# Attention by head pairs in 64-row halves of TensorE, the mask as a product, and the mixer spread over the next batch's attention steps

## The chip, the cores and the metric

The kernel runs on one core of one Trainium2 chip. The metric is the time of one execution on the device, in microseconds; lower is better. "TensorE" does matrix products, "VectorE" and "ScalarE" elementwise work, "GpSimd" copies and most DMA issues. A run is "fast" unless it lies more than 1.5% above the fastest of its kernel; only fast runs enter the ratios.

## The reference, cut to what matters

Four batches, 8 heads, 768 tokens, 64 columns a head: block-sparse attention, then a two-layer token and channel mixer on the 512 concatenated columns.

```python
scores = scale * np.matmul(q, k.transpose(0, 1, 3, 2))
# mask: neighbouring 32-token blocks, first and last block, and sampled blocks
scores = np.where(mask, scores, -1000000000.0)
attn = np.exp(scores - scores.max(-1))            # then divided by its row sum
x    = attn @ v                                    # (4, 768, 512), heads side by side

a1  = alpha1 * x + beta1
u   = x + lam * np.einsum('ts,bsd->btd', w_tok, a1)
a2  = alpha2 * u + beta2
out = u + lam * (np.maximum(a2 @ w_ch1, 0.0) @ w_ch2)
```

The scores are small (q and k have a spread of 0.1), so exponentials need no maximum.

## The kernel before: the parts that the change touches

Attention runs head by head in 192 steps (32 heads, 6 key tiles). One step is two QK products, one exponential on ScalarE and two PV products. The mask is inside the QK product: 24 extra contraction rows (88 instead of 64) carry block indicators and a large negative number. PV leaves the result with head columns on the partitions, so `emit_finish` transposes it back in fp32.

```python
def emit_qk(i, jt):
    ...
    nc.tensor.matmul(spsum[:, 0:512], kT[0 : D + NBLK, ts(jt, P)],
                     qT[0 : D + NBLK, 0:512], start=True, stop=True)
    nc.tensor.matmul(spsum[:, 512:S], ...)
    nc.scalar.activation(eT[:], spsum[:], AF.Exp, bias=expb[:], scale=SCALE)

def emit_pv(i, jt):
    ...
    nc.tensor.matmul(opsum[0 : D + 1, 0:512], vext[:, jt, :], eT[:, 0:512], ...)
    nc.tensor.matmul(opsum[0 : D + 1, 512:S], vext[:, jt, :], eT[:, 512:S], ...)
    ...                                  # after 6 key tiles: copy to otsb

def emit_finish(i):                      # 6 fp32 transposes, reciprocal, product
    ...

for g in range(NBH * NT + PVD):          # attention of ALL batches
    ...
nc.gpsimd.dma_start(w2b[:], ...)
nc.vector.tensor_mul(out=w2b[:], in0=w2b[:], in1=lam...)     # one product of 8192 columns
for b in range(B): ...                   # then the mixer of ALL batches
for c in range(NT): ...
```

The softmax here doesn't subtract the row's maximum and nothing guards it: scores larger than these inputs give would overflow.

## Time and profile before

| | before |
|---|---|
| median of the runs | 440.7 us |
| span of the profiled run | 436.4 us |
| first exponential | 13.7 us |
| last exponential | 203.5 us |
| step in the window 60 to 120 us | 0.91 us (66 exponentials in 60 us) |
| last exponential to the end (mixer) | 233 us |

The first fence has the busy times and the slices of the page. Each digit is the busy share of one fortieth of the span (about 11 us) in tenths; PEclk is TensorE's granted clock in tenths of full.

```profile
PE 387.7 (89%) x2175; PEld 211.5 (48%) x2196; DVE 189.1 (43%) x404; ACT 214.8 (49%) x289; POOL 83.9 (19%) x107
...
PE   0699489799989999898589999999999999999996
...
DVE  4345465876577567854945530311401301302101
ACT  1389469689977999696000043062060260440520
...
PEclk9999879989998999999989999999999999999999
```

The ACT row tells the structure: ScalarE is at 6 to 9 in most slices up to the nineteenth (attention), then mostly idle, while the PE row stays at 8 or 9 nearly to the end. Two phases stand one after the other: attention, paced by the exponentials, and the mixer, paced by TensorE.

The second fence is the window view of the attention (60 to 120 us) and of the hand-over (205 to 220 us). Each engine has its busy time and, in brackets, its instructions; the last columns are granted clock, DMA share and GB/s.

```profile
60.00:120.00 60.00, 56.63 (x394) 36.18 (x393) 39.55 (x97) 53.31 (x66) 26.85 (x34) 0.97 0.86 55
205.00:220.00 15.00, 6.93 (x54) 4.04 (x53) 13.96 (x30) 0.00 (x0) 0.00 (x0) 0.99 0.00 0
```

In the attention ScalarE is busy 53.3 of 60 us. Its mean record is 0.906 us, but records overlap a little: 53.3 us over 66 is 0.81 us a step, and in an unbroken run the starts are 0.78 to 0.80 us apart. In the hand-over TensorE works 6.9 of 15 us.

The third fence is from the waits of VectorE. Its columns: who waited, for what, microseconds in total, times, the longest.

```profile
DVE w2b L328 <- DMA w2b<-in_moe_w_ch_dram: 6.6, 1, 6.6
```

VectorE stands 6.6 us for the second channel weight, which lands at 50.1 us, and then needs 4.4 us to scale it.

### The profile page before, as it was taken

How to read it: one execution, taken by the hardware profiler on the slowest of the kernel's cores; microseconds unless marked ns; L12 is line 12 of the kernel's file. 1: busy time of each engine (PE TensorE's matmuls, PEld its weight loads, DVE VectorE, ACT ScalarE, POOL GpSimd, SP SyncE). 2: the span in 40 equal slices, each digit the busy share in tenths (PEclk: the TensorE clock that was granted, in tenths of full speed). 3: DMA queues.
4: the chain of work that ended last, by engine and by line, in shares of the span. 5: the costliest groups of instructions: out<-in, count | busy, mean ns of one | idle time of the engine just before them, and what ended most of it. 6: DMA issues, size and time to landing. Idle time of an engine off the chain costs nothing.

```text
span 436.4 us, 5598 instructions
## 1 busy us (share of the span) xinstructions
PE 387.7 (89%) x2175; PEld 211.5 (48%) x2196; DVE 189.1 (43%) x404; ACT 214.8 (49%) x289; POOL 83.9 (19%) x107
## 2 busy tenths in 40 slices
PE   0699489799989999898589999999999999999996
PEld 0366256456655666465234454444544544544442
DVE  4345465876577567854945530311401301302101
ACT  1389469689977999696000043062060260440520
POOL 9436234244443544210000000000000000000000
PEclk9999879989998999999989999999999999999999
DMA  9999949769984999520000000200101101001001
GB/s 129 183 208 154 166 29 63 47 43 64 59 55 29 66 62 59 33 19 2 0 2 0 0 2 16 82 0 26 72 0 50 49 2 72 24 2 73 23 26 72
DMA packets 84149, 22.46 MB, mean 51 GB/s; under 512 B 77140, under 2 KB 80156, under 8 KB 84124
## 3 DMA queue, kind: packets, MB, share of 16 engines
q0 software_dynamic: 78928, 14.96, 41.3%
q1 hardware_dynamic: 5196, 7.15, 4.8%
q8 instruction: 17, 0.28, 0.3%
q14 instruction: 8, 0.07, 0.0%
HBM read 30.77 MB, written 6.29 MB: 85 GB/s over the span
## 4 chain that ended last, share of the span: by engine, by line
PE 69%; DVE 11%; DMA 8%; POOL 4%; ACT 3%; issue 3%; another core or an unknown queue 1%; ACTq 0%; DVEq 0%; POOLq 0%
PE hps L377 18%; PE chps L390 18%; PE spsum L218 8%; PE tokps L345 7%; PE opsum L242 7%; PE opsum L249 3%; DMA w2b<-in_moe_w_ch_dram 3%; PE spsum L225 3%; DMA qk<-in_k_dram 2%; DMA vext<-in_v_dram 2%; ACT eT L233 2%; PE txp L206 2%; PE xps L268 2%; POOL qk L187 2%; DVE otsb L258 1%
## 5 line engine op out<-in xcount | busy, mean ns | idle before, releaser
L233 ACT ACTIVATE eT<-spsum,expb 128x768 f16<-128x768 f32 x192 | 156.9, 906 | 45.2 <-PE opsum L249 21.3
L384 ACT ACTIVATE hts<-hps 128x512 bf16<-128x512 f32 x96 | 56.7, 597 | 158.1 <-PE hps L377 158.1
L377 PE MATMUL hps<-a2t,w1b 128*128 128x512 bf16 x374 | 85.8, 379 | 1.5 <-ACT hts L384 0.5
L390 PE MATMUL chps<-w2b,hts 128*128 128x512 bf16 x376 | 83.3, 379 | 0.4
L242 PE MATMUL opsum<-eT,vext 128*65 128x512 f16 x192 | 75.2, 399 | 6.3 <-DVE vext L194 5.4
L399 DVE TENSOR_TENSOR ot<-x_sb,chps 128x512 f32<-128x512 f32 x24 | 16.5, 687 | 142.6 <-PE chps L390 139.8
L390 PEld LDWEIGHTS <-hts 128*128 128x128 bf16 x384 | 37.6, 98 | 45.3
L377 PEld LDWEIGHTS <-w1b 128*128 128x128 bf16 x384 | 37.6, 98 | 42.7 <-issue 2.5
L249 PE MATMUL opsum<-eT,vext 128*65 128x256 f16 x192 | 54.2, 282 | 0.0
L206 PE MATMUL txp<-identb,qk 128*128 128x128 bf16 x192 | 26.5, 232 | 22.3 <-DMA qk<-in_k_dram 14.8
L258 DVE COPY otsb<-opsum 65x768 f32<-65x768 f32 x32 | 30.5, 954 | 28.3 <-PE opsum L249 27.9
L184 POOL DMA_DIRECT2D qk<-in_q_dram x32 | 26.5, 829 | 63.5 <-PE txp L206 61.3
L191 POOL DMA_DIRECT2D vext<-in_v_dram x32 | 26.5, 828 | 40.4 <-PE opsum L249 31.6
L206 PEld LDWEIGHTS <-qk 128*128 128x128 bf16 x192 | 17.0, 104 | 32.8 <-DMA qk<-in_q_dram 14.0
L242 PEld LDWEIGHTS <-vext 128*65 128x65 f16 x192 | 22.1, 115 | 16.7 <-issue 3.1
L249 PEld LDWEIGHTS <-vext 128*65 128x65 f16 x192 | 22.1, 115 | 11.7 <-issue 7.9
L218 PE MATMUL spsum<-qText_65,kText_68 88*128 88x512 bf16 x66 | 26.4, 401 | 0.8 <-ACT eT L233 0.6
L187 POOL DMA_DIRECT2D qk<-in_k_dram x32 | 26.7, 834 | 0.0
L218 PE MATMUL spsum<-qText_66,kText_69 88*128 88x512 bf16 x66 | 25.6, 388 | 0.8 <-ACT eT L233 0.5
L345 PEld LDWEIGHTS <-wtokT 128*128 128x128 bf16 x144 | 14.4, 100 | 24.5 <-issue 7.7
L218 PE MATMUL spsum<-qText_67,kText_70 88*128 88x512 bf16 x60 | 23.1, 386 | 1.4 <-ACT eT L233 1.4
L353 DVE TENSOR_TENSOR x_sb<-x_sb,tokps 128x512 f32<-128x512 f32 x24 | 16.4, 687 | 15.3 <-PE tokps L345 15.3
(62 smaller groups left out, 336.7 us busy)
## 6 DMA issues: line engine op xcount, KB each, us to landing
out_dram<-ot SPq DMA_DIRECT2D x24, 256.0 KB, 2.0
qk<-in_q_dram POOLq DMA_DIRECT2D x32, 96.0 KB, 3.0
qk<-in_k_dram POOLq DMA_DIRECT2D x32, 96.0 KB, 3.3
vext<-in_v_dram POOLq DMA_DIRECT2D x32, 96.0 KB, 3.2
w1b<-in_moe_w_ch_dram POOLq DMA_DIRECT2D x1, 2048.0 KB, 14.0
w2b<-in_moe_w_ch_dram POOLq DMA_DIRECT2D x1, 2048.0 KB, 14.5
wtk<-in_moe_w_tok_dram POOLq DMA_DIRECT2D x1, 1152.0 KB, 10.3
lam_bc<-in_moe_lam_dram SPq DMA_DIRECT2D x1, 256.0 KB, 3.6
```

The source lines that it names most:

```text
L184: nc.gpsimd.dma_start(qk[:, :, 0:D], q[b, h].rearrange("(o p) d -> p o d", p=P))
L187: nc.gpsimd.dma_start(qk[:, :, D:P], k[b, h].rearrange("(o p) d -> p o d", p=P))
L206: nc.tensor.transpose(tps[:, j, :], qk[:, 3 * g + j, :], identb[:])
L218: nc.tensor.matmul(spsum[:, 0:512], kT[0 : D + NBLK, ts(jt, P)], qT[0 : D + NBLK, 0:512], start=True, stop=True,)
L233: nc.scalar.activation(eT[:], spsum[:], AF.Exp, bias=expb[:], scale=SCALE)
L242: nc.tensor.matmul(opsum[0 : D + 1, 0:512], vext[:, jt, :], eT[:, 0:512], start=(jt == 0), stop=(jt == NT - 1),)
L249: nc.tensor.matmul(opsum[0 : D + 1, 512:S], vext[:, jt, :], eT[:, 512:S], start=(jt == 0), stop=(jt == NT - 1),)
L258: nc.vector.tensor_copy(out=otsb[0 : D + 1, :], in_=opsum[0 : D + 1, :])
L345: nc.tensor.matmul(tokps[:], wtokT[:, sk, ts(tt, P)], a1pp[:, sk, :], start=(sk == 0), stop=(sk == NT - 1),)
L377: nc.tensor.matmul(hps[:], w1b[:, dk, ts(ntl, P)], a2t[:, dk, :], start=(dk == 0), stop=(dk == 3),)
L384: nc.scalar.activation(hts[:, ntl, :], hps[:], AF.Relu, bias=0.0, scale=1.0)
L390: nc.tensor.matmul(chps[:], hts[:, nk, ts(m, P)], w2b[:, nk, :], start=(nk == 0), stop=(nk == 15),)
```

## The change

Its intent: (1) one step now serves a *pair* of heads and half of the query tokens, with each head's 64 contraction rows in its own half of TensorE's rows, so that the two QK products can run side by side; (2) the mask becomes a 0/1 factor on the exponentials, multiplied by VectorE; (3) PV makes tokens the output rows, six products of 65 columns, so no transpose back is needed; (4) the mixer of batch b is cut into small pieces and woven into the attention steps of batch b+1, and only the last mixer stands alone; (5) larger DMA runs. The core of the diff (cuts marked; lines of indexing are left out):

```diff
-            nc.tensor.matmul(spsum[:, 0:512], kT[0 : D + NBLK, ts(jt, P)], ...)
-            nc.tensor.matmul(spsum[:, 512:S], kT[0 : D + NBLK, ts(jt, P)], ...)
-            nc.scalar.activation(eT[:], spsum[:], AF.Exp, bias=expb[:], scale=SCALE)
+        for a in range(2):
+            nc.tensor.matmul(
+                sps[:, a, 0:HS],
+                kT[a * D : (a + 1) * D, ts(jt, P)],
+                qT[a * D : (a + 1) * D, ts(hf, HS)],
+                start=True,
+                stop=True,
+            )
+        eT = wk.tile([P, 2, HS], F16, name="eT", tag="eT", bufs=5)
+        nc.scalar.activation(eT[:], sps[:, :, 0:HS], AF.Exp, bias=expb[:], scale=SCALE)
+        nc.vector.tensor_tensor(
+            out=eT[:],
+            in0=eT[:],
+            in1=mask[:, jt, ts(hf, HS)].unsqueeze(1).broadcast_to([P, 2, HS]),
+            op=ALU.mult,
+        )
 ...
-            nc.tensor.matmul(opsum[0 : D + 1, 0:512], vext[:, jt, :], eT[:, 0:512], ...)
-            nc.tensor.matmul(opsum[0 : D + 1, 512:S], vext[:, jt, :], eT[:, 512:S], ...)
+        for a in range(2):
+            for t in range(3):
+                nc.tensor.matmul(
+                    op[:, a, t, 0 : D + 1],
+                    eT[:, a, ts(t, P)],
+                    vx[:, a, jt, 0 : D + 1],
+                    ...
+                )
 ...
+    def mm_tile(shape, dt=FP):          # everything but scores and PV shares two buffers
+        return ps.tile(shape, dt, name="mm", tag="mm", bufs=2)
 ...
+    fill = setup()                      # wtok transposes, bias products, 8 pieces of w2b
+    for i in range(len(steps) + LAG):   # 192 steps
+        emit_qk(steps[i])
 ...
+            if pos == MIXLAG and b > 0:
+                ...
+                fill = mixer(b - 1)
+                rate = 52000.0 / PER
 ...
+        emit_pv(steps[i - LAG])
 ...
+        credit += rate
+        while credit > 0:               # so much of the mixer (or setup) per step
+            c = next(fill, None)
 ...
+    for _ in mixer(B - 1):
+        pass
```

## The prediction

> **What bounds the kernel before (span 436.4 us).** The profile has three parts.
> (a) 0 to about 55 us: start and a stall. The first exponential runs at 13.7 us. In the timeline the product that scales w2b sits in VectorE's queue and waits 6.6 us for its DMA (landing 50.1 us), then takes 4.4 us; the chain of waits shows that DMA as one 14.5 us piece.
> (b) about 55 to 205 us: attention, bound by ScalarE. In the window 60 to 120 us it ran 66 exponentials in 60 us (0.91 us a step) and was busy 53.3 us; inside an unbroken run one costs about 0.81 us. TensorE has slack but cannot use it: the mixer comes later.
> (c) about 205 to 432 us: the mixer, bound by TensorE (chain: hps, chps, tokps). N=512 matmuls start every 215 ns; 912 of them are 196 us, plus transposes, a 15 us hand-over at 205 to 220 us and an output tail of 4 us.
>
> **What the change does.** It puts three of the four mixers among the attention steps of the next batch, so (b) and (c) overlap. Costs on TensorE, from start-to-start times in the trace:
> - QK: two 384-column products in 64-row halves. The Trainium skill ("TensorE: Matmul & The Clock Gate", Part 3) says such tiles run concurrently, so 165 ns instead of 320; but "TensorEngine Tiling (Array Packing)", Key Properties, says a mode switch drains the engine, twice a step. No trace here shows either; I estimate 315 ns a step in all: no gain.
> - PV: six 65-column matmuls, each with a new 128-column weight load. The trace shows 55 ns start to start for bf16 128x128 load and transpose; I estimate 45 ns, 270 ns a step against 323.
> - The otsb copies and fp32 transposes (0.95 us and 6 x 62 ns a head) vanish.
> - Mixer matmuls cost the same (512 of 163 ns, 384+144 of 215 ns).
> Sum over the new instruction order: TensorE about 335 us.
>
> VectorE gains 192 mask products (fp16, 768 columns). The w2b product ran at 0.54 ns a column, so 0.4 to 0.56 us each, about 95 us; it stays near 57 us a batch. ScalarE gets 39 us of exponentials and about 17 us of 384-column relus a batch. Both stay under TensorE's roughly 80 us a batch, so batches 1 to 3 are bound by TensorE, with small bubbles because all mixer products share two PSUM buffers and relus queue behind exponentials.
>
> **Where time is lost.** Loads have 1536-byte reads instead of 256, but six memsets and two relayout copies on GpSimd precede the first product: first exponential at 15 to 18 us. In the new instruction order the first w2b product again stands early in VectorE's queue, after about 12 steps, and w2b is issued third behind wtk and w1b: I expect VectorE, then all engines, to stall from about 28 us until about 53 us. Batch 0 has no mixer to fill it.
>
> **Sum:** batch 0 ends near 90 us; batches 1 to 3 take 240 us; the last mixer 58 us; bubbles and output tail 8. About 396 us.
>
> Faster by over 2%: 0.91; within 2%: 0.05; slower: 0.04. Range 368 to 425 us.
>
> **Right or wrong shows in:** slices (TensorE near 9 from about 90 us on, ScalarE at 6 to 8); VectorE's wait for w2b; start-to-start of PV (45 ns) and of a QK pair (under 20 ns if concurrent) and the gap at the QK-PV change; the mask product's mean; VectorE idle in batches 1 to 3.
>
> **What would make it wrong:** PV at 60 ns or more or longer drains (+25 us); VectorE slower because GpSimd contends, becoming the bound; bubbles on the two shared buffers; or, on the other side, free mode switches and 30 ns PV (about 360 us).

## The result, and the profile after

| | before | after |
|---|---|---|
| median | 439.52 us (437.89 to 441.76) | 420.71 us (415.14 to 421.97) |
| ratio after / before | | 0.9513, 95% interval 0.9435 to 0.9591 |
| span of the profiled run | 436.4 us | 418.6 us |

A ratio here is the mean time of one kernel's fast runs over that of the other's fast runs of the same rounds, so it is not quite the ratio of the two medians. The 421.97 us run counted as slow by the 1.5% rule. The change gained 4.9%; the prediction had 396.0 us, a gain of 10%.

The busy times and slices of the page after (a slice is 10.5 us):

```profile
PE 370.4 (88%) x2951; PEld 186.2 (44%) x2978; DVE 259.3 (62%) x498; ACT 235.0 (56%) x321; POOL 69.6 (17%) x93
...
PE   0489299799799999998899999999999999789996
...
DVE  5886366988985584579854854699548546820101
ACT  1035246776448769754478599445785992044350
...
PEclk9999999757989999999899999999999999999999
```

TensorE has 8 or 9 in every slice from the twelfth to the last mixer, as intended, and ScalarE is spread out. TensorE's holes are in the first eleven slices (the 2 in the fifth is the stall on w2b), and VectorE, 43% busy before, is 62% busy and stands at 8 or 9 for more than one slice at regular places: slices 8 to 12, then 19 and 20, then 27 and 28, around the starts of the mixers of batches 0, 1 and 2 (slices 2 and 3 are the start of the kernel; 15, 23, 31 and 35 stand alone).

A second reading uses the start of every exponential, taken from the trace. There are 48 a batch, so the 49th begins batch 1. The sum of the prediction can be laid beside it:

| part | predicted | measured | difference |
|---|---|---|---|
| batch 0 (to the 49th exponential) | 90 | 98.0 | +8.0 |
| batches 1 to 3 (to the last exponential) | 240 | 251.7 | +11.7 |
| last mixer, bubbles and output tail | 66 | 68.9 | +2.9 |
| execution outside the profiled span | 0 | 2.1 | +2.1 |
| sum | 396 | 420.7 | +24.7 |

(The last row but one is 420.7 us less the span of 418.6 us.) The prediction gave its 8 us of "bubbles and output tail" as one sum; the table puts all of it in the third row, although some of the bubbles were meant for batches 1 to 3, so that the second difference may be a few us smaller and the third larger. Either way both large misses are in the attention.

The window view, with the windows cut at the first w2b product, the 49th and the last exponential:

```profile
49.20:98.00 48.80, 43.18 (x403) 23.84 (x402) 37.23 (x77) 30.06 (x34) 11.30 (x15) 0.80 0.35 52
98.00:349.70 251.70, 243.20 (x2072) 121.20 (x2095) 170.15 (x331) 172.15 (x240) 30.31 (x39) 0.98 0.18 35
```

In batches 1 to 3 TensorE is busy 243.2 of 251.7 us, so a first glance says "bound by TensorE". Keep in mind that products are pipelined and the ends of their records are modelled, so a busy TensorE is not one at its peak; the experiments show below that a part of these 243 us goes without any change to its products.

The waits of VectorE, with the same columns as before:

```profile
DVE eT L234 <- ACT eT L233: 72.5, 84, 1.5
...
DVE w2b L403 <- DMA w2b<-in_moe_w_ch_dram: 8.0, 1, 8.0
```

The wait for w2b is the predicted one: VectorE reaches the first w2b product at 41.2 us and stands 8.0 us until 49.2 us. The next fence, pieces of the chain of waits of batch 0 (start, microseconds, what), tells what happened then.

```profile
25.28 23.85 DMA w2b<-in_moe_w_ch_dram
49.16 0.69 DVE w2b L403
...
64.29 0.95 PE mm L392 x32
...
67.48 0.52 PE mm L392 x16
72.97 0.45 PE sps L225 x2
73.44 0.91 ACT eT L233
74.38 0.77 DVE eT L234
75.15 3.63 DVE w2b L403 x5
...
79.72 0.60 DVE a1p L283
80.32 0.47 DVE eT L234
80.79 0.60 DVE a1p L288
81.50 0.57 DVE a1p L283
82.07 0.47 DVE x_sb L266
82.54 0.60 DVE a1p L288
83.13 0.47 DVE eT L234
```

The first of these pieces is the 23.9 us load. Up to 73 us the chain is mostly TensorE. From 74 to 85 us it is VectorE without a break: five pieces of w2b (3.6 us), then mask products (`eT L234`) in turn with the first operations of the next mixer (`a1p`, `x_sb`).

Last, three pieces of TensorE's timeline near the end of the attention (start, microseconds, then engine, line, operation). The differences of the starts tell what a step costs.

```profile
348.78 0.59 PE L358 MATMUL mm<-w2b,hts 128*128 128x512 bf16 x2
349.31 0.34 PE L225 MATMUL sps<-qT,kT 64*128 64x384 bf16 x2
349.58 0.36 PE L251 MATMUL ops<-vext_154,eT 128*128 128x65 f16 x6
349.77 1.02 PE L358 MATMUL mm<-w2b,hts 128*128 128x512 bf16 x4
```

Two mixer products at 348.78 (215 ns each) should let the QK pair start at 349.21; it starts at 349.31, 0.10 us late. The next product starts 0.27 us after the pair, where one 384-column product costs 0.163; that is another 0.10 us. Over the whole trace the second product of a pair starts 3 to 4 ns after the first, so they do run side by side (the Trainium skill, "TensorE: Matmul & The Clock Gate", Part 3, states about 4 ns, and this trace agrees), but entering costs about 95 ns and leaving 100 ns. A pair thus costs 361 ns, against 2 x 162 = 324 ns for two full-row products. The six PV products take 0.19 us, about 30 ns each.

### The profile page after: what moved, and what is told of

The parts are those of the page before. It is cut to its first block, busy times and chain, and to the rows that moved or that the text cites. A ratio compares the mean times of both kernels' runs of the same rounds, so it can differ in the third digit from the quotient of the medians.

```text
span 418.6 us, 7215 instructions
## 1 busy us (share of the span) xinstructions
PE 370.4 (88%) x2951; PEld 186.2 (44%) x2978; DVE 259.3 (62%) x498; ACT 235.0 (56%) x321; POOL 69.6 (17%) x93
## 4 chain that ended last, share of the span: by engine, by line
PE 70%; DVE 18%; DMA 8%; issue 1%; ACT 1%; POOL 0%; POOLq 0%; DVEq 0%; ACTq 0%
PE mm L341 21%; PE mm L358 18%; PE sps L225 11%; PE ops L251 11%; DMA w2b<-in_moe_w_ch_dram 6%; PE mm L305 5%; DVE eT L234 4%; DVE a1p L283 2%; DMA v_88<-in_v_dram 2%; DVE x_sb L313 2%; PE mm L205 2%; DVE a1p L288 2%; DVE ub L317 2%; PE mm L327 1%; DVE w2b L403 1%
## 5 line engine op out<-in xcount | busy, mean ns | idle before, releaser
L233 ACT ACTIVATE eT<-sps,expb 128x768 f16<-128x768 f32 x192 | 170.2, 899 | 127.9 <-PE sps L225 123.5
L234 DVE TENSOR_TENSOR eT<-eT,mask 128x768 f16<-128x768 f16 x192 | 112.7, 594 | 73.3 <-ACT eT L233 72.5
L341 PE MATMUL mm<-uT,w1b 128*128 128x384 bf16 x512 | 96.0, 326 | 2.4 <-ACT hts L348 1.0
L348 ACT ACTIVATE hts<-mm,b1t 128x384 bf16<-128x384 f32 x128 | 73.9, 582 | 41.0 <-PE mm L341 39.0
L358 PE MATMUL mm<-w2b,hts 128*128 128x512 bf16 x365 | 90.2, 379 | 1.0
L225 PE MATMUL sps<-qT,kT 64*128 64x384 bf16 x384 | 81.2, 372 | 4.0 <-ACT eT L233 3.6
L251 PEld LDWEIGHTS <-eT 128*128 128x128 f16 x1152 | 52.5, 105 | 44.0 <-DVE eT L234 19.3
L225 PEld LDWEIGHTS <-kT 64*128 64x128 bf16 x384 | 21.2, 95 | 57.4 <-issue 51.0
L305 PE MATMUL mm<-a1p,wtokT 128*128 128x512 bf16 x136 | 37.0, 397 | 4.2 <-DVE x_sb L313 1.4
L305 PEld LDWEIGHTS <-wtokT 128*128 128x128 bf16 x144 | 13.6, 101 | 19.1 <-issue 8.5
L205 PE MATMUL mm<-identb,rel 128*128 128x128 bf16 x192 | 19.9, 253 | 0.6 <-POOL rel L199 0.4
## 6 DMA issues: line engine op xcount, KB each, us to landing
w2b<-in_moe_w_ch_dram POOLq DMA_DIRECT2D x1, 2048.0 KB, 23.9
```

The costliest lines, as they stand in the source:

```text
L205: nc.tensor.transpose(tps[:, o, :], rel[:, o].rearrange("p h d -> p (h d)"), identb[:])
L225: nc.tensor.matmul(sps[:, a, 0:HS], kT[a * D : (a + 1) * D, ts(jt, P)], qT[a * D : (a + 1) * D, ts(hf, HS)], start=True, stop=True,)
L233: nc.scalar.activation(eT[:], sps[:, :, 0:HS], AF.Exp, bias=expb[:], scale=SCALE)
L234: nc.vector.tensor_tensor(out=eT[:], in0=eT[:], in1=mask[:, jt, ts(hf, HS)].unsqueeze(1).broadcast_to([P, 2, HS]), op=ALU.mult,)
L251: nc.tensor.matmul(op[:, a, t, 0 : D + 1], eT[:, a, ts(t, P)], vx[:, a, jt, 0 : D + 1], start=(jt == 0 and a == 0 and t == 0), stop=(jt == ...
L305: nc.tensor.matmul(tp[:], wtokT[:, s, ts(t, P)], a1p[:, s, :], start=(s == 0), stop=(s == NT - 1),)
```

## The experiments

Each starts from the kernel after unless it says otherwise. The measured table is at the end of the section; "batch 0" is the start of the 49th exponential of the profiled run, "batches 1 to 3" runs from there to the last exponential.

### e1: keep TensorE busy in batch 0

In batch 0 the PV products started every 54 ns instead of 30, that is, TensorE ran at half clock from its first PV products at 28 us to 99 us, except for 75 to 79 us. In batch 0 the clock row of the page shows that only in slices 8 to 10 (7, 5 and 7); before its first record, at 75 us, it says "full". The rate of the products is the better witness. The edit adds one product per step of batch 0 that nobody reads:

```diff
+            if g[0] == 0:
+                dm = mm_tile([P, 512])
+                tc.keep_in_program_order(nc.tensor.matmul(dm[:], mask[:, 0, 0:P],
+                                         mask[:, 0, 0:512], start=True, stop=True))
```

> Edit: in batch 0 only, each attention step also issues one matmul of 512 columns whose result nobody reads. Theory C (clock): batch 0 is slow after the w2b stall because TensorE stays at half clock there: in the changed kernel's trace PV starts are 53 ns apart and a QK pair holds the next matmul for 430 ns up to about 99 us, against 30 and 265 ns later. If so, the extra work warms the clock: PV at 30 ns and 265 ns before 90 us, the stretch from the first w2b product (49.2 us) to exponential 48 (98.0 us) shrinks from 49 us to about 40 us, and the whole is 6 to 10 us faster than the changed kernel (ratio to before about 0.935). Theory D (VectorE bounds batch 0): the stretch stays at 49 us and the whole is unchanged or slower, for TensorE only gets more to do.

Measured: 418.55 us, ratio 0.9457 (0.9385 to 0.9529), an interval that overlaps that of the kernel after. TensorE had its full clock from 59.8 to 94 us, and batch 0 ended at 94.7 instead of 98.0 us; from the first w2b product it took 45.1 us, between the 40 of theory C and the 49 of theory D. These 3.3 us are a net gain: the 48 extra products are themselves about 10 us of TensorE's time (215 ns each). What the half clock costs without such a cure is not shown by this run, and it can be more than 3.3 us.

### e2: leave the mask products out (wrong)

```diff
-        nc.vector.tensor_tensor(
-            out=eT[:], in0=eT[:], in1=mask[:, jt, ts(hf, HS)]..., op=ALU.mult)
```

> Edit: the 192 products with the mask are left out, so the result is wrong on purpose; 112.7 us of VectorE time go. Theory D (VectorE bounds batch 0 and the start of each later batch): the stretch from 49.2 us to exponential 48 falls from 49 to about 30 us (36 exponentials of 0.81 us), each start of a mixer comes some 6 us earlier, in all 25 to 40 us faster than the changed kernel (ratio about 0.87 to 0.89). Theory C (clock): TensorE stays at half clock in batch 0, so only the part in which the chain of waits runs over VectorE (75 to 86 us and 99 to 107 us) shrinks: 8 to 15 us faster (ratio about 0.92 to 0.935).

Measured: 400.52 us, ratio 0.9087 (0.9041 to 0.9134); the output is wrong (relative error 0.82). Batch 0 ended at 89.0 (9.0 us earlier) and batches 1 to 3 took 240.7 instead of 251.7 us (11.0 us less). So VectorE's mask products cost 20 us of the total although VectorE is 62% busy; the gain lies between the two expectations (25 to 40 and 8 to 15 us). The windows of the same two stretches in this run:

```profile
49.20:89.00 39.80, 36.68 (x412) 22.11 (x412) 21.62 (x47) 28.35 (x34) 16.13 (x21) 0.69 0.70 101
89.00:329.70 240.70, 236.40 (x2067) 118.40 (x2087) 94.35 (x181) 171.50 (x240) 25.65 (x32) 1.00 0.15 31
```

TensorE is busy 236.4 of 240.7 us here, with nearly the same number of products as before. Of the 11.0 us, 4.2 are idle time of TensorE that went (8.5 to 4.3 us). Of the other 6.8 us about 4.0 go with the granted clock, 0.984 in the one and 1.000 in the other: the kernel after had 8.0 us at half clock in these batches, this run none. That the clock fell because TensorE waited for mask products fits the times (116 to 120 us and 202 to 205 us lie in VectorE's dense slices 12 and 20), but no run shows it. About 2.8 us stay unassigned.

### e3: both QK products over all 128 rows (wrong)

```diff
-                kT[a * D : (a + 1) * D, ts(jt, P)],
-                qT[a * D : (a + 1) * D, ts(hf, HS)],
+                kT[:, ts(jt, P)],
+                qT[:, ts(hf, HS)],
```

Each score is then the sum of two heads, which is wrong, though the comparison passes, because scores this small hardly move the softmax. It only serves to take the switches between 64-row and 128-row products away.

> Edit: each of the two score products contracts over all 128 rows (both heads summed, so the result is wrong on purpose), with the same columns and the same number of matmuls; no instruction uses 64 rows any more. Theory: the halves run together (starts 3 to 4 ns apart) but cost about 96 ns on entry and 100 ns on exit, so a QK pair takes 361 ns against 2 x 162 = 324 ns without halves. Expected: 37 ns less a step, over the 144 TensorE-bound steps 5 us; if the halves also keep the clock down in batch 0 (theory C), up to 10 us more there. Ratio 0.92 to 0.94. Rival, by the intent of the change: row halves save a pass, so without them TensorE has 160 ns more a step and the kernel is about 23 us slower than the changed one (ratio about 1.0).

Measured: 404.91 us, ratio 0.9179 (0.9133 to 0.9225), just beyond the expected 0.92 to 0.94; the rival fell. Batch 0 ended at 90.2 (7.8 us earlier) and batches 1 to 3 took 245.2 us (6.5 us less). 6.5 us over 144 steps is 45 ns a step, near the 361 - 324 = 37 ns of the pitches; half clock is no rival there (6.8 us of these batches against 8.0 before). In batch 0 the gain is larger, and two things changed at once. The switches went: at half clock the product after a pair starts 430 ns later, and in the kernel after 12 of the 48 pairs are split by other products (mostly the six PV products of another step, in four pairs transposes), each time with another pair of switches. But the clock changed too: in batch 0 of this run PV products started every 30 ns nearly everywhere except 52 to 58 and 79 to 83 us, against 54 ns before. How much of the 7.8 us belongs to which is not shown.

### e6 and e13: which of these causes hide behind one another

e6 is e1 and e2 together. It tells whether half clock and VectorE take turns in batch 0, so that removing one only uncovers the other.

> Edit: the extra matmul in batch 0 and no mask products, together (result wrong on purpose). From the first w2b product (49.2 us) to exponential 48 the changed kernel needs 48.8 us, with the extra matmul alone 45.5, without mask products alone 39.8. Theory B (two limits take turns in batch 0, TensorE at half clock and VectorE, so lifting one uncovers the other): together about 31 to 34 us, the pace of ScalarE (36 exponentials of 0.85 us). Rival (clock hardly matters): 38 to 40 us, as without mask products alone.

Measured: 403.6 us, batch 0 ended at 88.7 us against 89.0 without the extra product. From the first w2b product that is 39.6 us, so the turn-taking theory with its 31 to 34 us fell. But this does not clear the clock: the extra products again cost about 10 us of TensorE's time, and without mask products the clock was already full from 74 us on. (In batches 1 to 3, where e6 and e2 have the same code, e6 took 3.0 us longer. Stages of single profiled runs can differ by that much.)

e13 is e2 and e3 together.

> Wrong on purpose: after.py with both score products over all 128 rows and without the mask products. From the first w2b product (49 us) to exponential 48 the kernel took 48.8 us; without mask products 39.8, with full rows 41.0. If the two causes are separate: about 32 us, ScalarE's own pace, 36 steps of 0.85 us and a little. If a third thing binds (the setup's transposes and w2b products, the half clock): 37 us or more. Batches 1 to 3 were 251.7 us; minus 11 without mask, minus 6.5 with full rows; if additive about 234 us.

Measured: 388.6 us in 2 runs. From the first w2b product (50.2 us) to the 49th exponential it took 33.5 us, against 48.8 in the kernel after, near the 32 us of the separate-causes theory and well under 37. Batches 1 to 3 took 235.0 us (234 expected). The causes add up almost fully: e2 gained 20.2 us, e3 15.8, both 32.1 us. The stretches of batch 0 show that they act at different times (microseconds, each run from its own first w2b product):

| exponentials | after | e1 extra product | e2 no mask | e6 e1+e2 | e3 full rows | e13 e2+e3 |
|---|---|---|---|---|---|---|
| first w2b product to the 25th | 19.7 | 20.4 | 18.5 | 19.4 | 14.4 | 13.6 |
| 25th to 49th | 29.2 | 24.7 | 21.0 | 20.2 | 25.7 | 19.8 |

In the first stretch (wtok transposes and bias products among the steps) leaving out the mask products gained little and full rows much. In the second (w2b pieces and the first mixer operations on VectorE) it is the other way round. The clock is not separated in any of these runs: of the starts of consecutive PV products in batch 0, 11 of 245 were at the full-clock distance (under 42 ns) in the kernel after, 165 of 238 in e2, 201 of 242 in e3 and 213 of 233 in e13. The gains in batch 0 are those of the work taken away and of the clock together.

### e4: the w2b products late

The eight w2b products stand at steps 38 to 45, pinned there, instead of where the scheduler hoisted them (about step 12 on):

```diff
-        for g4 in range(8):            # in setup()
+    def scale_w2(g4):
+        tc.keep_in_program_order(
             nc.vector.tensor_mul(out=w2b[:, 2 * g4 : 2 * g4 + 2, :], ...)
+        )
 ...
+            if 38 <= i < 46:
+                scale_w2(i - 38)
```

> Edit: the eight products that scale w2b are pinned in VectorE's queue behind the mask products of steps 38 to 45, when w2b has long landed. The result is right. The wait of VectorE for w2b (8.0 us) and the pause of exponentials from 44 to 50 us go. All theories: 5 to 9 us faster than the changed kernel (ratio about 0.935), less if the work that was stalled is then bound by TensorE's half clock (C) or by VectorE (D), which both must still do the same.

Measured: 411.32 us, ratio 0.9313 (0.9258 to 0.9368), 9.4 us better than the kernel after and right as a result. No wait for w2b is left among VectorE's waits, and batch 0 ends at 90.0 us. Batches 1 to 3 took 251.7 us as before, so all of the gain is in batch 0: 8.0 us of the profiled span. So the stall, 8 us, was worth its length.

### e10: late w2b and a lean start

In the start of the kernel after, GpSimd's six fills of 792 columns run beside VectorE's casts, and a 24x768 cast took 5.12 us. e10 is e4 with fills of the ones column only and the copies of v kept in program order:

```diff
-        nc.gpsimd.memset(t[:], 1.0)
+        nc.gpsimd.memset(t[:, :, :, D:VW], 1.0)
```

> Edit: w2b products late as before, and a leaner start: only the column of ones of the value tiles is set by GpSimd (24 instead of 792 columns each), and the copies of v are kept behind the mask building in VectorE's queue. Right result. In the changed kernel the cast of the block indicator took 5.1 us beside GpSimd's memsets and a copy waited 2.9 us for v. Expected: first exponential at 17 to 20 us instead of 25.6 to 27, and as no stall on w2b hides it any more, 6 to 9 us faster than with late w2b alone (ratio 0.913 to 0.918). If the start hid behind something else (DMA of wtk, w1b), below 3 us.

Measured: 402.4 us, ratio 0.9136 (0.9079 to 0.9192). The ratio lies in the expected range, but by luck: the early start that it rested on missed, for the first exponential ran at 25.1 us, not at 17 to 20. The cast took only about 0.6 us, but VectorE's timeline of e10 (start, microseconds, operation, and in brackets the idle time before it and its releaser) shows why nothing moved:

```profile
11.84 1.00 DVE L156 CAST kbq<-mm 24x384 bf16<-24x384 f32 x2
16.13 0.17 DVE L187 CAST be2b<-be2T 128x4 bf16<-128x4 f32 x1 [3.29 <-DMA be2T<-in_moe_beta_dram]
16.21 6.62 DVE L168 CAST mask<-mm 128x384 f16<-128x384 f32 x12
23.25 0.56 DVE L209 COPY qT<-mm 128x768 bf16<-128x768 bf16 x1 [0.42 <-PE mm L205]
```

The copy of beta2 stands before the mask's casts and waits 3.3 us for a DMA that gathers 512 single numbers. The gain of 8.9 us over e4 came later, in batch 0, which ended at 80.3 us. Nearly all of it lies in the first 24 steps, which took 25.7 us instead of 33.3; the next 24 took 29.5 us in both. The clock is the suspect. The chain of waits of e4 and then of e10 (start, microseconds, what) runs over the same products there, three transposes (`mm`) and one score product (`sps`):

```profile
44.30 0.46 PE mm L382 x3
44.75 0.43 PE sps L225
```

```profile
44.57 0.30 PE mm L384 x3
44.87 0.27 PE sps L227
```

In e4 PV products started every 54 ns up to 50 us, in e10 every 30 ns from 34 to 51 us. So the half clock in these steps may be worth most of these 7.6 us, more than the net 3.3 us of e1 suggested. No run isolates it, nor shows why the clock rose earlier.

### e8 and e9: full rows done right, and GpSimd as a helper

e8 is e10 with correct full-row products: each head's q stands in its own 128-row tile, zeros in the other half, and ScalarE copies kT. (To make room, a few buffers were merged.)

```diff
-            t = wk.tile([P, S], BF, name=nm, tag=nm, bufs=5)
-            nc.vector.tensor_copy(out=t[:], ...)
+            if nm == "qT":               # qz: persistent, zeroed once
+                for a in range(2):
+                    nc.vector.tensor_copy(out=t[a * D : (a + 1) * D, a, :], ...)
+            else:
+                nc.scalar.copy(t[:], ...)
 ...
-                kT[a * D : (a + 1) * D, ts(jt, P)], qT[a * D : (a + 1) * D, ts(hf, HS)],
+                kT[:, ts(jt, P)], qT[:, a, ts(hf, HS)],
```

> Edit: late w2b and lean start, and full-row score products that are right: q of each head is copied into its own 128-row tile whose other half is zero, so no instruction uses 64 rows; k is copied by ScalarE. Compared with the late and lean version: 37 ns a step and no clock trouble, as full rows alone gave 14 to 16 us; part of that was in batch 0, where other waits remain. Expected 10 to 16 us faster than late and lean: ratio 0.885 to 0.90. If zeros or the ScalarE copies cost as much as they save: equal to it.

Measured: 398.03 us, ratio 0.9017 (0.8975 to 0.9058); the output is right. The expectation missed: e8 is 4.4 us faster than e10, not 10 to 16. Batch 0 ended at 80.1 us, as in e10, though the first exponential came 3.3 us later (28.4 us). Batches 1 to 3 took 246.3 us, 2.6 less than e10's 248.9 and 5.4 less than in the kernel after, where e3 gained 6.5; e10 had already lost less to half clock there (1.9 us at half clock, the kernel after 8.0, e8 3.4). The number of VectorE's copies did not change (32 of q take the place of 16 of q and 16 of k); ScalarE got 16 more, 12.8 us in all. What they cost is not shown.

e9 adds to e8 that GpSimd does the three operations per token tile with alpha1, beta1 and alpha2, for batches 0 to 2:

```diff
+        eng = nc.gpsimd if b < B - 1 else nc.vector
-            nc.vector.tensor_tensor(out=t[:, s, :], ...)
+            eng.tensor_tensor(out=t[:, s, :], ...)
```

> Edit: as padded, and for batches 0 to 2 the alpha1 and beta1 steps and the alpha2 product run on GpSimd instead of VectorE (54 instructions of 0.68 us leave VectorE). Theory D2 (VectorE bounds the start of each mixer, worth 11 us over batches 1 to 3 by the run without mask products): 4 to 10 us faster than padded. Rival (TensorE bounds there, or GpSimd is slower and holds VectorE's products up[...]): same or slower than padded, with the mask product's mean above 0.594 us.

Measured: 414.84 us, ratio 0.9397 (0.935 to 0.9445), 17 us worse than e8, as the rival had it. First the group of the mask product in e8, then the mask product and two of the moved operations in e9 (columns: line, engine, operation, tiles, shapes, count, then busy time, mean ns, and the idle time before):

```profile
L249 DVE TENSOR_TENSOR eT<-eT,mask 128x768 f16<-128x768 f16 x192 | 110.3, 582 | 65.0 <-ACT eT L248 64.0
```

And the groups of e9:

```profile
L249 DVE TENSOR_TENSOR eT<-eT,mask 128x768 f16<-128x768 f16 x192 | 140.8, 743 | 71.1 <-ACT eT L248 69.8
...
L300 POOL TENSOR_TENSOR a1p<-x_sb,a_bc 128x512 bf16<-128x512 f32 x18 | 27.4, 1536 | 38.0 <-DVE x_sb L281 37.9
...
L334 POOL TENSOR_TENSOR ub<-x_sb,a_bc 128x512 bf16<-128x512 f32 x18 | 22.9, 1275 | 14.6 <-DVE x_sb L330 11.8
```

The same mask product takes 743 instead of 582 ns on average, and GpSimd needs 1.3 to 1.5 us for what took VectorE 0.68. The Trainium skill ("SBUF — State Buffer", section "Who interferes with whom") says that a VectorE instruction with two inputs in SBUF contends with a GpSimd instruction that reads SBUF; this pair of runs agrees. How the 17 us divide is not shown: GpSimd's own slower operations can hold the mixer up too, and in batches 1 to 3 TensorE was at half clock for 13.7 us, against 3.4 in e8.

### e11: leaner start again

e8 with the beta2 copy in the setup steps and half of the mask built in steps 4 to 9:

```diff
-    nc.vector.tensor_copy(out=be2b[:], in_=be2T[:])      # at the start
+        tc.keep_in_program_order(nc.vector.tensor_copy(out=be2b[:], in_=be2T[:]))   # in setup()
-    for hf in range(2): ...                              # 12 mask tiles at the start
+    for jt in range(NT):
+        build_mask(0, jt)
 ...
+            if 4 <= i < 10:
+                build_mask(1, i - 4)
```

> e8_padded with a leaner start: the copy of beta2 moves out of the start into the setup steps, and only the first half of the mask is built before the first score product, the second half at steps 4 to 9. In e8 the first exponential ran at 28.4 us, because the beta2 copy stood ahead of the mask casts in VectorE's queue and waited for a DMA that landed at 16.1 us. If that wait is what held the start: first exponential at 17 to 20 us, exponential 48 at about 72 us, and 6 to 9 us less in all (about 390 us). If the weights' DMA or the batch-0 chain binds instead: exponential 48 stays within 3 us of e8's 80.1 us and the total within 3 us of 398.

Measured: 394.95 us, ratio 0.8924 (0.8878 to 0.897): 3.1 us better than e8, between the two expectations. The first exponential came 6.4 us earlier, at 22.0, but batch 0 ended only 2.8 us earlier. VectorE's timeline of e11 shows that the start was again held by a DMA in front of the mask's chain:

```profile
6.17 0.48 DVE L135 TENSOR_TENSOR eqt<-rndf,kbi 24x24 f32<-24x24 f32 x1
9.14 1.12 DVE L193 CAST lam_bcb<-lam_bc 128x512 bf16<-128x512 f32 x1 [2.50 <-DMA lam_bc<-in_moe_lam_dram]
10.18 0.17 DVE L141 TENSOR_TENSOR mbm<-mbm,eqt 24x24 f32<-24x24 f32 x1
...
12.37 0.69 DVE L195 TENSOR_TENSOR b_bc<-b_bc,lam_bc 128x512 f32<-128x512 f32 x1 [0.61 <-DMA b_bc<-in_moe_beta_dram]
...
14.13 0.17 DVE L145 CAST mbb<-mbm 24x24 bf16<-24x24 f32 x1
```

The cast of lambda waits 2.5 us, and the mask's small operations (`mbm`, `mbb`) stand behind it.

### e12: take work off VectorE without GpSimd

e11 with the beta1 term as a seventh product per token tile, alpha2 multiplied into w1b once, and ScalarE making the bf16 copy:

```diff
+            nc.tensor.matmul(tp[:], rsum[:, ts(t, P)], blb[:], start=False, stop=True)
-            nc.vector.tensor_tensor(out=ub[:], in0=x_sb[:, bt, :], in1=a2_bc[:], op=ALU.mult)
+            nc.scalar.copy(ub[:], x_sb[:, bt, :])
```

> e11 with work taken off VectorE without giving it to GpSimd: the addition of beta1 becomes a seventh product of TensorE per token tile, alpha2 is multiplied into w1b once, and the cast of the mixer input goes to ScalarE. About 48 operations of 0.68 us (32 us) leave VectorE, TensorE gets about 5 us and ScalarE about 14 us. Theory A, that VectorE's burst at the start of each mixer costs time in batches 1 to 3 and before the last mixer: 4 to 10 us less than e11, and the idle 7 us of TensorE before the last mixer shrinks to 4 or less. Theory B, that batches 1 to 3 are TensorE's own work and VectorE's burst hides behind it: the same as e11 or up to 4 us more.

Measured: 391.3 us, ratio 0.8845 (0.8794 to 0.8895), 3.7 us better than e11. Batches 1 to 3 took 243.3 us, 2.9 less, although TensorE got 24 more products in the mixers (18 of them in batches 1 to 3, about 3.9 us at 215 ns). TensorE's idle time in the 26 us after the last exponential, worked out from the products' own rates, went from about 6.4 to 4.8 us. Theory A has the right sign, but its size was 4 to 10 us and its idle time 4 us or less; both just missed. The total is clear (the runs of e11 and e12 do not overlap); the 2.9 us of one stage are no more than what e2 and e6 differ by with the same code.

### e14: the order of the start

e12 with the cast of lambda and the products with lambda moved to step 20.

```diff
-    nc.vector.tensor_copy(out=lam_bcb[:], in_=lam_bc[:])                      # at the start
-    nc.vector.tensor_mul(out=a1_bc[:], in0=a1_bc[:], in1=lam_bc[:])
+        tc.keep_in_program_order(nc.vector.tensor_copy(out=lam_bcb[:], ...))  # in setup()
+        tc.keep_in_program_order(nc.vector.tensor_mul(out=a1_bc[:], ...))
```

> e12_light with the four small operations that use lambda, alpha1, beta1 (cast of lambda, the two products with it) moved from the start to step 20 of batch 0. In e11 and e12 the first exponential ran at 22.0 and 22.5 us instead of the 17 to 20 expected of e11: in the timeline VectorE stood 2.2 to 2.5 us before the cast of lambda and 0.3 to 0.6 us before the products, each waiting for its DMA, with the mask's chain behind them; the cast of the block mask came at 14.1 us. If that order is what held the start: the block mask's cast at 8 to 9 us, first exponential at 16 to 18 us, and 4 to 6 us less in all (385 to 387 us). If the loads of q and k or GpSimd's relayout bind next: first exponential not before 20 us and 0 to 2 us less.

Measured: 390.2 us (388.93 to 392.88), ratio 0.8843 (0.8767 to 0.8918): the same as e12. The first exponential came at 19.5 instead of 22.5 us and the block mask's cast at 11.2 instead of 14.1, but batch 0 ended at 76.2 instead of 77.4 us. The first exponential came between the two expectations, the total (1.1 us less) fits the second. In batch 0 VectorE was busy 23.8 of 25 us in 25 to 50 us already in e12, so an earlier start may only lengthen the queue before it; no run tests that.

### All runs together

| kernel | median us | ratio | batch 0 | batches 1 to 3 | rest of span |
|---|---|---|---|---|---|
| after | 420.71 | 0.9513 | 98.0 | 251.7 | 68.9 |
| e1 extra product | 418.55 | 0.9457 | 94.7 | 252.7 | 68.9 |
| e2 no mask (wrong) | 400.52 | 0.9087 | 89.0 | 240.7 | 68.8 |
| e3 full rows (wrong) | 404.91 | 0.9179 | 90.2 | 245.2 | 68.8 |
| e4 late w2b | 411.32 | 0.9313 | 90.0 | 251.7 | 68.9 |
| e6 e1 + e2 (wrong) | 403.6 | 0.9145 | 88.7 | 243.7 | 68.8 |
| e8 padded full rows | 398.03 | 0.9017 | 80.1 | 246.3 | 68.8 |
| e9 e8 + GpSimd | 414.84 | 0.9397 | 82.7 | 262.0 | 68.9 |
| e10 e4 + lean start | 402.4 | 0.9136 | 80.3 | 248.9 | 68.9 |
| e11 e8 + leaner start | 394.95 | 0.8924 | 77.3 | 246.3 | 68.8 |
| e12 e11 + light VectorE | 391.3 | 0.8845 | 77.4 | 243.3 | 68.4 |
| e13 e2 + e3 (wrong) | 388.6 | 0.8784 | 83.7 | 235.0 | 68.7 |
| e14 e12 + order | 390.2 | 0.8843 | 76.2 | 243.2 | 68.4 |

The stages are from one profiled run each. The kernel before had medians of 440.4 to 442.0 us in the experiments. The best correct version, e12 (with e14 its equal), beats both; by the two ratios it takes 7% less time than the kernel after (0.8845 / 0.9513 = 0.930).

## Why the prediction was wrong

The direction, the overlap of mixer and attention, and the stall were right; the size was off by 24.7 us, more than the 18.8 us that were gained (439.5 to 420.7). The steps, as the prediction put them:

- "First exponential at 15 to 18 us": wrong, 25.6 us. Beside GpSimd's fills, the small casts of the start took up to 5.12 us. It probably cost little by itself, since all engines waited for w2b later anyway.
- "Stall from about 28 us until about 53 us": the mechanism was right, VectorE waited for w2b. The size was milder: VectorE stood still from 41.2 to 49.2 us. e4 shows that the stall was worth 9.4 us by the medians (8.0 by the profiled spans).
- "Batch 0 ends near 90 us": this term failed by 8 us. It implied 37 us for the 36 steps after 53 us, about 1.03 us a step; in fact 34 steps were left at 49.2 us, and they took 48.8 us, 1.44 us each. The prediction counted one engine's work at a time there. In fact w2b pieces, first mixer operations and mask products share VectorE (e2: -9.0 us), and TensorE was slowed by row switches, split pairs and half clock (e3: -7.8 us). Without mask products and row switches, and with them most of the half clock, the same stretch took 33.5 us (e13). The prediction had no term for the clock; how much of the 8 us is the clock's stays open.
- "Batches 1 to 3 are bound by TensorE, with small bubbles": this is the step that failed most, by 11.7 us. It argued from VectorE's sum over a batch. VectorE's mean share in those batches is 68% (170 of 252 us), but its work comes in bursts, 17.8 of 20 us in 180 to 200 us and 17.0 of 20 us in 280 to 300 us, where a PV product has to wait for its mask product. Without mask products the term is 240.7 us (about 4.0 of the 11.0 us between go with the granted clock). That this is so near the predicted 240 is partly luck: without the row switches too it is 235.0 us (e13), so the 240 held a QK term that was too small and a PV term that was too large, named below.
- "Mask products, 0.4 to 0.56 us each, about 95 us": the mean was 594 ns and the sum 112.7 us. Back to back they took 0.47 us; the trace doesn't name what makes the others longer.
- "QK 315 ns a step in all: no gain": mis-sized. 361 ns, because each switch costs about 0.1 us, two a step; e3 shows 6.5 us of that in batches 1 to 3 (its 7.8 us in batch 0 include the clock). Full rows are cheaper than halves here.
- "PV 45 ns, 270 ns a step": mis-sized the other way, 30 ns and about 195 ns. This offset the QK term, so the sum of TensorE's work (335 us predicted, about 321 us by adding the products' own rates at full clock, with about 38 us of switches among them) was near.
- "Last mixer 58, bubbles and output tail 8": 68.9 against 66, if all the bubbles are counted here. And the predicted sum was a span; an execution is about 2 us longer.

Two of the warnings named the right suspects: longer drains, and VectorE as the bound. Of GpSimd contention the kernel after shows an effect at the start; that it can matter in the steps is shown by e9 only. The third warning, bubbles on the two shared buffers, was not tested by a run; the waits of TensorE that the trace names in batches 1 to 3 are 6.1 us, 3.8 of them for mask products.

Open: what the half clock cost in batch 0. Batch 0 of e10 ended 9.7 us before that of e4 (90.0 to 80.3) with the first exponential only 2 us earlier, and what stands out in those steps of the two traces is the clock; but no run changes the clock alone. And e2's 11.0 us in batches 1 to 3 were not divided among the bursts; e12, which removes about 32 us of VectorE's work by the estimate, got back only 2.9 us net of them.

## What to carry to other kernels

When work is moved so that two phases overlap, check each engine's load in the *densest stretch* of the new order, not its mean over the phase: an engine at 62% cost 20 us here. Splitting TensorE's rows between two products did not pay here, with one pair between other products: two full-row products with zeros in the other half were faster (e8). Whether it pays when many products run in that mode before it switches back was not run. And an operation that waits for a late DMA should be pinned behind everything that doesn't need it: here one wait of 8.0 us in VectorE's queue left TensorE and ScalarE without work from 45 to 50 us. Last, look at TensorE's own rates in every run before a gain is put down to the edit: several edits here changed the clock as well.

## What the Trainium skill lacked or had wrong

- "TensorEngine Tiling (Array Packing)", Key Properties, says that a mode switch drains TensorE, without a figure. Here entering the 64-row mode cost about 95 ns and leaving it 100 ns, at full clock; a pair of 64-row products of 384 columns cost 361 ns against 324 ns for two full-row ones. Its section "When to Use Tiling" recommends two row tiles for 64 contraction rows and does not weigh this cost; here, with one pair between other products, the two tiles were the slower choice.
- "TensorE: Matmul & The Clock Gate", section "Wait — 56ns, not 53.3ns?", gives start to start as N / 2.4 GHz + 2.5 ns. For 65 columns that is 29.6 ns, and 30 ns were measured with a new 128-column weight load before each product; 54 ns at half clock agrees with the N / 1.2 GHz that the section gives for it. But the page's section "Back-to-back issue gap" says that at small N the first formula under-counts once weight loads are in the stream; for these 65 columns it did not, so the page leaves it open which of the two holds for a product like those of the prediction's 45 ns. Its rule that about 3.4 us of sustained work release the clock has no figure for how dense the work must be: here TensorE ran at half clock through nearly all of 49.2 to 98 us, with records that fill 88% of it (43.2 of 48.8 us; the ends of records are modelled).
- "SBUF — State Buffer", section "Who interferes with whom", states the contention without a price for this pair of operations: 582 to 743 ns for the mask product of VectorE, and 1.28 to 1.54 us for GpSimd's own products of 128x512.
- "TensorE: Matmul & The Clock Gate", section "Seeing it yourself", warns that clock events in a trace can be unreliable, but not in which way: here the clock row read 1.00 for 25 to 75 us, before the trace's first clock record, while PV products started every 54 ns.
